# DeltaNet and a SiLU feed-forward layer in one kernel: chunk 0's norms, transposes, loads and scores rearranged

## The chip, the core and the metric

The kernel runs on one NeuronCore of a Trainium2 chip. The core has five engines that run their own instruction streams and meet at semaphores: TensorE (PE, matrix multiplication into PSUM; its weight loads appear as PEld), VectorE (DVE), ScalarE (ACT), GpSimd (POOL) and SyncE (SP), which here only issues DMA transfers. The metric is the time of one execution on the device in microseconds (us), as the median of several runs.

## What is computed

For each of 32 heads (batch 4, 8 heads, 768 tokens, head size 48), the keys are normalized and a 48x48 state is updated token by token:

```python
k_n = k / (norm(k) + 1e-6)
for t in range(S):
    y[t] = q[t] @ state
    state += beta[t] * outer(k_n[t], v[t] - k_n[t] @ state)
```

The result, seen as 3072 tokens of 384 numbers, goes through a feed-forward layer: `h = x @ w_in` (384 to 2048), `g = h * sigmoid(h)`, `out = g @ w_out` (2048 to 384). The two weight matrices arrive as 64-bit floats and are narrowed on the chip.

## The kernel before

**Chunks.** The 768 tokens are cut into six chunks of 128. In a chunk the token loop is replaced by matrices: the scores of keys against keys (`ap0`) and of keys against queries (`ap1`, masked to be causal), the inverse of a triangular matrix made of beta and the key scores, and products with the values. For the inverse each head's 128 tokens are split into four blocks of 32, so that DVE holds 128 blocks, one per partition, and inverts them all by rank-one updates. Chunk 0 has its own form, `invert_first` (L660): it inverts only the two 16x16 corners of each block, in 15 steps of two instructions (`rank`, L677, and the addition, L681), and then multiplies by beta over the squared norm, in the code `step` (L684).

**Joining the blocks.** DVE then turns the inverse twice: `low` (L691, 512 elements per partition) and `up` (L695, 1024). PE joins the corners to blocks of 64: `corner` (L718, which reads `low`), `turned` (L734, reads `up`), `straight` (L747, reads `up`), `merge_half` (L807). Between them ACT and DVE copy PSUM out (L545 is a copy by ACT and L548 one by DVE, whatever the tile); L725 on DVE adds the diagonal after `corner`. This runs as `joins(0)` for the first 64 tokens of the chunk and later, among other work, as `joins(1)` for the others.

**What comes ahead of it in chunk 0.** Keys are loaded by `load_k` (L142, six DMAs). POOL squares them (`square`, L385), DVE sums (`add_squares`, L389), and `norm_steps` finds the norm: a seed from the bits (L403), three Newton rounds (L409, L412, L413), the norm (L417, L418), its reciprocal (L419), times beta (L420), and four instructions for `spread` (L423), one per block of 32 rows. PE sums `spread` into place (`block_steps`, matmul `pg`, L446) and ACT copies it to `step` (L451). Meanwhile PE transposes the keys (`turn`, L501; evacuated by DVE in L513 or ACT in L515), forms the 32x32 blocks of scores (`first_blocks`, L1292), and DVE brings them to one block per partition with one transpose (`blocks_in`, L1299). The first product of the inverse is L669. beta is transposed by PE and copied by ACT (`beta_of`, L361 and L364).

**Orders written out by hand.** `pin` chains each compute instruction behind the one before on its engine, so every engine's order is the order of the Python text. `in_line` chains all DMAs of SP in the same way; within `deep`, each of them also waits for the end of the transfer two before it. An entry in the list `pace` makes the next DMA wait for one more instruction. `busy` issues a matmul `pw` (L348, 128x128 by 384) whose result nobody reads. In chunk 0, a list of words says what PE gets after which step of the inverse: `s2` is the key scores of batch 2, `u0` the transposes of the queries of batch 0, `w0` the query scores. After the joins, a long script of words orders everything until PE's feed-forward matmuls (`phid`, L1049) fill it; `narrow` (L232, L233 on ACT, L237, L241 on DVE, L245 on POOL) turns a piece of the weights to 32 bits.

**The SP queue before** holds, in this order: keys of chunk 0, queries of chunk 0 (tile `z`), pieces 0 and 1 of `w_in` (tile `raw`), keys of chunk 1, values of chunk 0 (`vf`), piece 2 of `w_in` (in the room of `w_out`), queries of chunk 1 (in the room of `sums_of_g`), pieces 4, 3, 6, 5 of `w_in`.

## Time and profile before

| | |
|---|---|
| median of 3 runs | 642.78 us (641.49 to 644.65) |
| the profiled execution's own time | 643.75 us |
| its span in the profile | 642.0 us |
| mean granted TensorE clock | 0.975 |
| instructions | 21886 |
| PE, DVE, ACT, POOL busy | 621.0, 402.2, 216.8, 94.5 us |
| read from and written to memory | 39.62 MB, 10.49 MB |

The profile is of one execution. A row of the timeline gives the start in us, the time from the first to the last instruction of a merged group, the engine, the line, what is written and read, the count, and in brackets how long the engine had been idle and which event ended that. "issue" there means that the profile shows nothing it waited for. PE's matmuls of 32-bit numbers appear twice each in the counts. A row of the windows gives the length of a stretch, the busy time of each engine in it with the number of instructions, the granted clock (1 is full speed), the share of DMA time and the GB/s.

### The profile page before, as it was taken

What the parts mean: (1) busy time and instruction counts of PE and PEld (TensorE: products, weight loads), DVE (VectorE), ACT (ScalarE), POOL (GpSimd) and SP (SyncE); (2) the same over time, 40 slices, a digit from 0 to 9 for tenths busy, and PEclk for the clock granted to TensorE, in tenths of its full rate; (3) what the DMA queues carried; (4) which work ended last, traced back from release to release, by engine and by line L of the source; (5) the groups of instructions that cost most, each with busy time, mean ns of one, the idle gap of its engine ahead of it and who ended that gap; (6) DMA issues with size and microseconds to landing.
All of it is one profiled execution on the core that took longest, in us unless ns stands there. A gap on an engine that the chain in (4) does not pass through costs nothing.

```text
span 642.0 us, 21886 instructions
## 1 busy us (share of the span) xinstructions
PE 621.0 (97%) x9642; PEld 547.7 (85%) x9642; DVE 402.2 (63%) x917; ACT 216.8 (34%) x512; POOL 94.5 (15%) x96
## 2 busy tenths in 40 slices
PE   6879999999999999999999999999999999999997
PEld 4767788666799978999989999989989989989997
DVE  5845888998774986564975563987563974212112
ACT  2655765251351122452122451122451122441120
POOL 5322730246010020010020010020002000000000
PEclk9758999999999999999999999999999999999999
DMA  9855454160369334269233269324173024100101
GB/s 171 184 120 186 146 123 106 50 149 3 84 127 158 59 76 49 59 135 160 39 92 43 48 137 147 60 75 61 29 148 80 1 74 61 38 16 1 26 0 26
DMA packets 141695, 53.69 MB, mean 84 GB/s; under 512 B 113296, under 2 KB 135056, under 8 KB 141600
## 3 DMA queue, kind: packets, MB, share of 16 engines
q1 hardware_dynamic: 141264, 52.14, 39.8%
q8 instruction: 76, 1.25, 0.8%
q10 hardware_dynamic: 336, 0.15, 0.1%
q14 instruction: 19, 0.16, 0.1%
HBM read 39.62 MB, written 10.49 MB: 78 GB/s over the span
## 4 chain that ended last, share of the span: by engine, by line
PE 71%; DVE 11%; DMA 7%; SPq 6%; issue 2%; ACT 2%; POOL 0%; DVEq 0%; POOLq 0%
PE phid L1049 27%; PE px L1156 13%; PE py L1156 10%; PE po L1084 7%; DVE rank L628 4%; DVE x L633 3%; PE pz L841 2%; PE pa L530 2%; PE ph L829 2%; SPq L142 2%; SPq L197 2%; PE pyc L922 2%; PE pyc L909 2%; DVE sums_of_g L1138 1%; PE pu L861 1%
## 5 line engine op out<-in xcount | busy, mean ns | idle before, releaser
L1049 PE MATMUL phid<-xT,w_in 128*128 128x256 f32 x1152 | 258.9, 383 | 0.1
L1049 PEld LDWEIGHTS phid<-xT,w_in 128*128 128x128 f32 x1152 | 217.0, 191 | 30.7 <-issue 1.3
L1059 ACT ACTIVATE gT<-phid 128x512 f32<-128x512 f32 x88 | 52.6, 598 | 143.1 <-PE phid L1049 136.5
L628 DVE SCALAR_TENSOR_TENSOR rank<-g,step,x 128x31 f32<-128x31 f32 (+15 forms) x124 | 49.8, 401 | 36.9 <-DMA g<-blocks 33.5
L1138 DVE TENSOR_TENSOR sums_of_g<-gT 128x384 f32<-128x384 f32 (+1 forms) x60 | 29.7, 514 | 56.7 <-ACT gT L1059 46.1
L1156 PE MATMUL py<-w_out,sums_of_g 128*128 128x192 f32 x320 | 56.8, 329 | 0.0
L1156 PE MATMUL px<-sums_of_w,sums_of_g 128*128 128x192 f32 x320 | 56.6, 329 | 0.0
L1156 PEld LDWEIGHTS px<-sums_of_w,sums_of_g 128*128 128x128 f32 x320 | 52.2, 190 | 0.5
L1156 PEld LDWEIGHTS py<-w_out,sums_of_g 128*128 128x128 f32 x320 | 52.2, 190 | 0.4
L633 DVE TENSOR_TENSOR x<-x,rank 128x31 f32<-128x31 f32 (+15 forms) x124 | 42.5, 343 | 4.3
L468 POOL TENSOR_TENSOR vf<-vf,n_slot 128x768 f32<-128x768 f32 x10 | 14.7, 1482 | 173.2 <-DMA vf<-in_v_dram 173.1
L868 DVE TENSOR_TENSOR state<-state,pu 48x384 f32<-48x384 f32 x44 | 24.3, 552 | 21.0 <-PE pu L861 20.0
L545 ACT COPY xT<-pyc 48x128 f32<-48x128 f32 (+2 forms) x126 | 32.7, 260 | 1.7
L489 DVE STREAM_TRANSPOSE kq<-stage 128x512 f32<-128x512 f32 x28 | 28.3, 1116 | 4.7 <-DMA stage<-in_q_dram 4.6
L1156 PE MATMUL px<-sums_of_w,gT 128*128 128x192 f32 x160 | 28.4, 329 | 0.0
L1156 PE MATMUL py<-w_out,gT 128*128 128x192 f32 x160 | 28.4, 329 | 0.0
L1156 PE MATMUL px<-w_out,gT 128*128 128x192 f32 x160 | 28.0, 327 | 0.0
L841 PEld LDWEIGHTS pz<-vf,xi 64*64 64x64 f32 x768 | 25.0, 142 | 3.2 <-issue 2.2
L551 POOL COPY g<-x 64x256 f32<-64x256 f32 x4 | 5.0, 1243 | 152.1 <-DVE x L636 152.1
L1156 PEld LDWEIGHTS px<-w_out,gT 128*128 128x128 f32 x160 | 26.4, 190 | 0.5
L841 PE MATMUL pz<-vf,xi 64*64 64x48 f32 x768 | 26.6, 226 | 0.0
L1156 PEld LDWEIGHTS py<-w_out,gT 128*128 128x128 f32 x160 | 26.1, 190 | 0.3
(197 smaller groups left out, 827.7 us busy)
## 6 DMA issues: line engine op xcount, KB each, us to landing
vf<-in_v_dram SPq DMA_DIRECT2D x48, 96.0 KB, 2.9
out_dram<-o SPq DMA_DIRECT2D x42, 96.0 KB, 2.2
w_out<-in_moe_w_in_dram SPq DMA_DIRECT2D x12, 256.0 KB, 3.5
sums_of_w<-in_moe_w_out_dram SPq DMA_DIRECT2D x8, 384.0 KB, 3.8
blocks<-ap SPq DMA_DIRECT2D x40, 64.0 KB, 1.9
g<-blocks SPq DMA_DIRECT2D x5, 512.0 KB, 3.8
kb<-in_k_dram SPq DMA_DIRECT2D x12, 192.0 KB, 4.6
kb<-in_k_dram SPq DMA_DIRECT2D x24, 96.0 KB, 4.5
```

The source lines that it names most:

```text
L468: pin(nc.gpsimd.tensor_tensor(out=vf, in0=vf, in1=of, op=ALU.mult))
L489: pin(nc.vector.transpose(out=kqs[c, b][:, :, j, :].rearrange("p a (i m) -> p a m i", i=T), in_=src.rearrange("p a (m d) -> p a m d", d=D) ...
L545: return pin(nc.scalar.copy(to, of))
L628: pin(nc.vector.scalar_tensor_tensor(out=tv, in0=g[:, 0:m, m : m + 1].to_broadcast([P, m, n]), scalar=step[:, m : m + 1], in1=x[:, m : m + ...
L633: yield pin(nc.vector.tensor_tensor(out=x[:, 0:m, m:T], in0=x[:, 0:m, m:T], in1=tv, op=ALU.add))
L841: yield pin(nc.tensor.matmul(pz[rows, n * D : (n + 1) * D], lhsT=xis[g][rows, u * H + 2 * p + e, :], rhs=vfs[c][rows, hf, g * HB + u, p, : ...
L868: pin(nc.vector.tensor_tensor(out=to, in0=to, in1=by_heads(pu[of]), op=ALU.add))
L1049: pin(nc.tensor.matmul(ph[:, j * GT : (j + 1) * GT], lhsT=w_in[:, a, (2 * f + j) * P : (2 * f + j + 1) * P], rhs=xTs[c, hf][:, a, :], star ...
L1059: pin(nc.scalar.activation(out=hidden_of(c, hf, f), in_=ph[:], func=ACTF.Silu, scale=-0.5 if in_blocks(c) else 0.5))
L1084: pin(nc.tensor.matmul(pos[i][:, 0:DM], lhsT=hidden_of(0, hf, f // 2)[:, at : at + C], rhs=w_outs[f // HFF][:, f % HFF, :], start=(f == 0) ...
L1138: pin(nc.vector.tensor_tensor(out=sums_of_g[:, k, fs], in0=of[0], in1=of[1], op=op))
L1156: pin(nc.tensor.matmul(to, lhsT=at, rhs=quarter(f, *b) if isinstance(b, tuple) else sums_of_w[b][:, f], start=start and f == 0, stop=f == ...
```

## The change

All of it is in chunk 0, except that the norm's formula is shared by all chunks.

- `norm_steps`: another seed constant, one Newton round with other constants and one cubic round, of which the norm itself comes out. Chunk 0 then squares the norm, takes the reciprocal, and multiplies `spread` by it in one instruction of 128x128; ACT has put minus beta into `spread` ahead of that in four copies (`beta_of`). The other chunks keep their reciprocal and their five instructions behind it.
- The square of the last batch's keys goes from POOL to ACT.
- The two clearings of `xi` on POOL go ahead of the squares.
- The two transposes write `low` and `up` in order; `corner`, `turned` and `straight` read them with a stride of 32 numbers.
- Queries of chunk 0 are issued later in the text, and their first DMA waits for the sums of the third batch (`pace`). Values of chunk 0 go between pieces 0 and 1 of `w_in`, ahead of the keys of chunk 1.
- The key scores of batch 0 go ahead of the norms' `pg` on PE, those of batch 1 behind `blocks_in`; the word list of the inverse is another one; the narrowing of piece 0 begins at its eleventh step.
- Four more `pw` matmuls in all: eight instead of four. One is ahead of the last batch's `first_blocks`, one ahead of `pg` behind the scores of batch 0, one ahead of the scores of batch 1, and two are among the inverse's steps; the one behind the scores of batch 1 is gone.

The core of the diff:

```diff
-    load_q(0)
...
-        pin(nc.scalar.activation(
-            out=beta_tok[:, c, :].rearrange("p (n e) -> p e n", e=2),
-            in_=pb[:, 0:BH].rearrange("p (e n) -> p e n", e=2), func=ACTF.Copy,
-        ))
+        for j in range(NB if c == 0 else 1):
+            rows = slice(T * j, T * (j + 1)) if c == 0 else ALL_ROWS
+            to = spread[rows, j, :] if c == 0 else beta_tok[:, c, :]
+            pin(nc.scalar.mul(
+                to.rearrange("p (n e) -> p e n", e=2), pb[rows, 0:BH].rearrange("p (e n) -> p e n", e=2),
+                -1.0 if c == 0 else 1.0,
+            ))
...
+        if (c, b) == (0, 3):
+            pin(nc.scalar.activation(out=squared[c, b], in_=kb, func=ACTF.Square))
+        else:
+            pin(nc.gpsimd.tensor_tensor(out=squared[c, b], in0=kb, in1=kb, op=ALU.mult))
...
-        for _ in range(3):
-            yield pin(nc.vector.scalar_tensor_tensor(
-                out=t, in0=ss, scalar=-0.5, in1=root, op0=ALU.mult, op1=ALU.mult
+        yield pin(nc.vector.scalar_tensor_tensor(out=t, in0=ss, scalar=-k, in1=root, op0=ALU.mult, op1=ALU.mult))
+        yield pin(nc.vector.tensor_tensor(out=t, in0=t, in1=root, op=ALU.mult))
+        yield pin(nc.vector.scalar_tensor_tensor(
+            out=r, in0=t, scalar=k * 2.38924456, in1=root, op0=ALU.add, op1=ALU.mult
+        ))
+        yield pin(nc.vector.scalar_tensor_tensor(out=t, in0=ss, scalar=0.5, in1=r, op0=ALU.mult, op1=ALU.mult))
+        yield pin(nc.vector.tensor_tensor(out=root, in0=t, in1=r, op=ALU.mult))
+        yield pin(nc.vector.scalar_tensor_tensor(
+            out=r, in0=root, scalar=-5.0 / 3.0, in1=root, op0=ALU.add, op1=ALU.mult
+        ))
+        yield pin(nc.vector.scalar_tensor_tensor(out=t, in0=r, scalar=1.25, in1=t, op0=ALU.add, op1=ALU.mult))
+        yield pin(nc.vector.tensor_scalar(
+            out=n[:], in0=t, scalar1=3.0, scalar2=1e-6, op0=ALU.mult, op1=ALU.add
+        ))
+        if c == 0:
+            yield pin(nc.vector.tensor_tensor(out=t, in0=n[:], in1=n[:], op=ALU.mult))
+            yield pin(nc.vector.reciprocal(out=r, in_=t))
+            yield pin(nc.vector.tensor_tensor(
+                out=spread[:], in0=spread[:], in1=r.unsqueeze(1).to_broadcast([P, NB, BH]), op=ALU.mult
             ))
...
-        low = sum_room[:, AT_LOW : AT_LOW + BH * Q].rearrange("p (n s) -> p n s", s=Q)
+        low = sum_room[:, AT_LOW : AT_LOW + BH * Q].rearrange("p (s n) -> p s n", s=Q)
-        pin(nc.vector.transpose(out=low.rearrange("p n s -> p s n"), in_=x[:, 0:Q, :]))
+        pin(nc.vector.transpose(out=low, in_=x[:, 0:Q, :]))
...
-                        rhs=low[rows[j], n, :], start=True, stop=True,
+                        rhs=low[rows[j], :, n], start=True, stop=True,
...
-    for b in range(B):
+    for t in xis:
+        pin(nc.gpsimd.memset(t, 0.0))
+    for b in range(3):
         square(0, b)
     block_room(0)
     for b in range(2):
         turn(0, b, 0, (A, CC)[b % 2], b % 2 == 0)
-    for b in range(B):
+    square(0, 3)
+    for b in range(2):
         add_squares(0, b)
-    for b in range(2):
         first_blocks(b)
     for b in range(2, B):
         turn(0, b, 0, (A, CC)[b % 2], False)
+        add_squares(0, b)
+        if b == 2:
+            pace.append(pins[seen_on])
     first_blocks(2)
     beta_of(0)
+    busy(1)
     first_blocks(3)
-    busy(0)
-    for t in xis:
-        pin(nc.gpsimd.memset(t, 0.0))
+    load_q(0)
+    first_score(0)
+    busy(1)
     first_sizes = norm_steps(0)
-    go(first_sizes, 18)
+    go(first_sizes, 12)
     step = block_steps(0)
     go(first_sizes, 99)
     blocks_in()
...
     fetch_w_in(0)
+    load_v(0)
     fetch_w_in(1)
     load_k(1)
-    load_v(0)
+    busy(1)
+    first_score(1)
     for c in range(1, NCH):
         beta_of(c)
-    for b in range(2):
-        first_score(b)
-    busy(1)
     fetch_w_in(2)
     deep(load_q, 1)
...
-    begin(("in", 0))
...
-        for word in ["s2 u0 u1", "", "w0", "s3", "w1", "u2", "", "u3 w2", "", "", "", "", "w3", "", "", "", "", "", "", "", "", ""][n].split():
+        for word in [
+            "s2", "n s3", "u0", "u1 w0", "w1", "u2", "u3", "w2", "w3", "n", "N", "", "", "", "", "", "",
+        ][n].split():
```

Here `n` is one `busy`, and `N` begins the narrowing of piece 0.

## The prediction

> **What bounds the kernel now.** I read the page first, then the windows by stage, then the timeline of the first 60 us.
>
> ```profile
> span 642.0 us, 21886 instructions
> PE 621.0 (97%) x9642; PEld 547.7 (85%) x9642; DVE 402.2 (63%) x917; ACT 216.8 (34%) x512; POOL 94.5 (15%) x96
> PEclk9758999999999999999999999999999999999999
> PE 71%; DVE 11%; DMA 7%; SPq 6%; issue 2%; ACT 2%; POOL 0%; DVEq 0%; POOLq 0%
> ```
>
> PE is busy for 97% of the span, and its clock is granted in full except in the first slices of 16 us. The windows (columns: length, PE, PEld, DVE, ACT, POOL busy, clock, DMA share, GB/s) say where the rest is.
>
> ```profile
> 17.60:26.20 8.60, 8.36 (x210) 6.70 (x209) 7.58 (x30) 6.47 (x18) 0.19 (x1) 0.67 0.92 157
> 30.10:47.00 16.90, 12.12 (x429) 11.49 (x431) 8.24 (x18) 7.68 (x16) 6.62 (x5) 0.50 0.53 138
> 47.00:60.00 13.00, 11.98 (x291) 10.26 (x285) 7.20 (x11) 7.68 (x14) 3.69 (x2) 0.89 0.54 164
> 120.00:642.00 522.00, 516.15 (x7158) 461.04 (x7156) 313.06 (x709) 152.36 (x374) 51.73 (x46) 1.00 0.37 71
> ```
>
> From about 47 us on PE is full, and the change leaves its work there as it is. So the change is worth as many us as PE enters that stage earlier. Ahead of it the order is keys, norms, inverse, joins, and up to the joins DVE carries it:
>
> ```profile
> 9.71 0.55 DVE L389 TENSOR_REDUCE ss<-sq 128x8 f32<-128x384 f32 x1 [0.89 <-POOL sq L385]
> 10.49 0.55 DVE L389 TENSOR_REDUCE ss<-sq 128x8 f32<-128x384 f32 x1 [0.23 <-POOL sq L385]
> 11.08 0.30 DVE L403 TENSOR_SCALAR seed<-ss 128x32 uint32<-128x32 uint32 x1
> 11.42 0.19 DVE L409 SCALAR_TENSOR_TENSOR nt<-ss,seed 128x32 f32<-128x32 f32 x1
> ...
> 13.46 0.19 DVE L417 TENSOR_TENSOR nt<-nr,ss 128x32 f32<-128x32 f32 x1
> ...
> 13.90 0.35 DVE L419 RECIPROCAL nr<-n 128x32 f32<-128x32 f32 x1
> 14.36 0.19 DVE L420 TENSOR_TENSOR nt<-nr,beta_tok 128x32 f32<-128x32 f32 x1
> 14.59 0.77 DVE L423 SCALAR_TENSOR_TENSOR spread<-nr,nt 32x32 f32<-32x32 f32 x4
> 15.39 1.25 DVE L1299 STREAM_TRANSPOSE sums_of_w<-blocks 128x1024 f32<-128x1024 f32 x1
> 16.75 0.69 DVE L669 TENSOR_TENSOR sums_of_w<-sums_of_w,step 128x512 f32<-128x512 f32 x1
> ...
> 21.89 0.29 DVE L681 TENSOR_TENSOR sums_of_w<-sums_of_w,rank 128x128 f32<-128x128 f32 x1
> ```
>
> No row of DVE from the seed to L669 has an idle time in brackets: one instruction behind the other sets the start of the inverse.
>
> **The change, part by part.** *The last square on ACT.* DVE's fourth sum came 0.23 us late behind POOL; with ACT squaring beside POOL it follows the third at once. Gain 0.23 us. The square is 384 elements per partition and goes where ACT was idle (first row below); if that cover is gone, L515 moves by about 0.45 us, half the 0.91 us that ACT needs for 768 elements (ACT, L232, further down).
>
> *Norms.* Now 18 instructions from 11.08 to 15.36 us (14.59 + 0.77), 4.28 us. After: 12. The seed takes 0.34 us to the next start; the nine starts from 11.42 to 13.46 give 0.227 us each, and nine of the other instructions are of that kind (2.04 us); the reciprocal takes 0.46 us (13.90 to 14.36); the product of 128x128 is bounded below by an instruction of 32 elements, 0.19 us, and above by two of L681, 0.6 us; I take L681 itself, the same size, 0.29 us and 0.03 to start. Sum 3.16 us, gain 1.12 us. Together DVE is ready 1.35 us earlier, at 14.0 us, and L669 could start at 15.4.
>
> *What stands in its way.* L669 also needs `step`, which PE and ACT make, and the change puts more ahead of that on PE.
>
> ```profile
> 9.87 1.07 ACT L515 COPY kq<-pt 128x512 f32<-128x512 f32 x2 [1.64 <-PE pt L501]
> 11.47 1.85 POOL L1328 MEMSET xi<- 128x1024 f32 x2
> 13.39 0.84 PE L1292 MATMUL blocks<-kq 48*32 48x32 f32 x58 [1.76 <-issue]
> 15.51 0.61 PE L446 MATMUL pg<-pick,spread 128*128 128x32 f32 x2 [1.28 <-DVE spread L423]
> 16.15 0.19 ACT L451 COPY step<-pg 128x32 f32<-128x32 f32 x1 [4.47 <-PE pg L446]
> 17.65 1.99 PE L530 MATMUL pa<-kq 48*64 48x64 f32 x64
> 19.56 1.65 PE L348 MATMUL pw<-state,ident 128*128 128x384 f32 x2
> 20.21 0.91 ACT L232 ACTIVATE w_in<-raw 128x768 f32<-128x768 f32 x1
> 34.05 0.69 PE L734 MATMUL pl<-sums_of_w 32*32 32x32 f32 x19 [2.01 <-issue]
> ```
>
> Behind the third batch's blocks (11.4 us) PE will issue `pw`, the last 64 block matmuls, the scores of batch 0, `pw`, `pg`. At the durations above, most of them under a halved clock, that is 1.65 + 0.93 (0.84 x 64/58) + 1.0 (half of L530) + 1.65 + 0.61 = 5.84 us, `step` at 17.5 us and L669 0.75 us later than now. If the stall of 1.76 us at 13.39 stays as well, it is 2.5 us later. At the full clock the 5.84 halve to 2.9, and DVE decides, 1.35 us earlier. I take the full clock for the first three (half of 3.58 us), as the window around them was granted it, the half clock for the rest, and no stall, because the queries no longer load at that time: 11.4 + 1.79 + 2.26 = 15.5, `step` at 15.8, L669 at about 15.95. **Gain 0.8 us**; ends +1.35 and -2.5.
>
> *Four copies of beta by ACT* take the place of one. They come after L515 and end by about 12.5 us, ahead of the product at 13.7: no cost, and up to 0.3 us if they don't. *The clearings of `xi`*, 1.85 us, go into POOL's wait for the keys; POOL also loses a square, so nothing waits for them.
>
> *The two transposes in order.*
>
> ```profile
> 27.23 1.06 DVE L691 STREAM_TRANSPOSE sums_of_w<-sums_of_w 128x512 f32<-128x512 f32 x1
> 28.15 1.91 DVE L695 STREAM_TRANSPOSE sums_of_w<-sums_of_w 128x1024 f32<-128x1024 f32 x1
> 29.94 1.45 DVE L725 SCALAR_TENSOR_TENSOR sums_of_w<-pl,second,pick 64x128 f32<-64x128 f32 x4
> 30.41 1.63 PE L734 MATMUL pl<-sums_of_w 32*32 32x32 f32 x40 [0.43 <-DVE sums_of_w L725]
> ```
>
> Written with a stride they take 2.1 and 1.9 ns per element. L1299, which writes in order and reads with a stride, takes 1.25 us for 1024, 1.2 ns each. So `low` goes to 0.62 us and `up` to 1.25: 1.10 us less, and L725 and the joins start that much sooner. If only the reading mattered, `up` would stay at 1.91 and the gain be 0.44; that is the case in which the change doesn't do what it says. **I take 1.1 us.** L725 can't start before `corner` is through, but that begins earlier too.
>
> *Strided reading on PE.* 640 of the matmul records (L718, L734, L747 in both joins) now read `low` or `up` with a stride of 32 numbers. No row shows PE reading SBUF with a stride; bounds are nothing, or less, and a doubling. I take nothing: these matmuls move 16 or 32 columns.
>
> *Loads.* The queries waited for nothing (5.98 us below); now they wait for the third sum, which ends at 10.26. All of SP's queue behind them slides by 4.3 us.
>
> ```profile
> 5.98 4.01 SPq L142 DMA_DIRECT2D z<-in_q_dram  x6
> ...
> 31.33 8.29 SPq L142 DMA_DIRECT2D sums_of_g<-in_q_dram  x6
> 39.67 8.06 SPq L292 DMA_DIRECT2D w_out<-in_moe_w_in_dram  x6
> w_out<-in_moe_w_in_dram SPq DMA_DIRECT2D x12, 256.0 KB, 3.5
> 47.65 0.47 PEld L501 LDWEIGHTS pt<-ident,sums_of_g 128*128 128x128 f32 x4
> 56.04 0.89 ACT L232 ACTIVATE w_in<-w_out 128x768 f32<-128x768 f32 x1
> ```
>
> Against 4.3 us of delay and 1.9 us of earlier use, 6.2 in all: the queries of chunk 1 are through in half at about 35 + 3 us and used at 47.65, 9 us of slack. Piece 3 of the weights, issued by 47.7 and landing 3.5 us later, is used at 56.04: 4.8 us, so ACT would wait 1.4 us for it. What is queued behind it on ACT is the rest of the narrowing and the activations of `phid`, which wait for PE anyway. I price it at nothing; 1.4 us if that cover is gone.
>
> *`pw`.* Two of the four added ones stand ahead of `pg` and are in the sum; the others lie under the inverse, where DVE is ahead of PE.
>
> **Sum:** 0.8 + 1.1 = 1.9 us from the profiled execution, whose span of 642.0 and the 1.73 us around it make 643.75; it becomes 641.85. That execution is 0.97 us above the median, so the forecast is 642.78 - 1.9 = **640.9 us**.
>
> **Rivals.** *Warm clock.* The joins ran at a clock of 0.50 (30.10 to 47.00). The same 320 instructions at the two clocks (same columns, DVE and ACT behind PE):
>
> ```profile
> 28.00:43.00 15.00, 6.03 (x320) 5.33 (x320) 3.92 (x10) 2.17 (x6) 0.57 0.58 141
> 50.00:70.00 20.00, 4.83 (x320) 4.06 (x320) 3.95 (x10) 2.17 (x6) 0.91 0.52 162
> ```
>
> They cost 1.2 us more in the first, and the other matmuls up to 47 us (some 6 us of busy time) could gain as much again. If the added `pw` hold the clock, 1 to 4 us come on top: 637 to 640 us, middle 638.4. Against it: the last `pw` stands at the tenth step, about 21 us, some five us ahead of the joins. The Trainium skill (TensorE: Matmul & The Clock Gate, Part 1) says that the clock is given after a busy window of about 3.4 us and taken after an idle one; by it the gap before the joins would cost the clock again, and the phase differs between runs. The trace agrees that the clock comes in stages, 0.67, 0.50, 0.89 in the windows.
>
> *PE ahead of `pg`.* The stall or the half clock holds `step`, and the norms' gain turns to a loss of up to 2.5 us: with the transposes 642 to 644.2 us. For it: both lie in the rows; against it: the queries are out of the way.
>
> *Strided reads, the slower side.* The records of one `joins` have 6.03 and 4.83 us, 10.9 in all. If strided reads lengthen them by more than a sixth (1.9 of 10.9), the gain is gone; by 47%, the kernel is 0.5% slower; doubled, it is 640.9 + 10.9 = 651.8. The Trainium skill (SBUF — State Buffer, Door 1: The DMA port swizzle, the note on cachelines) speaks against the change here: an access that leaves a 16-byte line for another pays a penalty, so that 32-bit numbers a stride of 32 apart would all pay. DVE's two transposes agree with it (1.06 us for 512), L1299's strided read does not, though it reads PSUM; for PE no run here shows it yet.
>
> *Late loads.* The 4.3 us reach ACT or the joins where I saw slack: 642 to 645.
>
> **How the numbers follow.** Forecast 0.47 (639.6 to 642), warm clock 0.22, PE ahead of `pg` 0.13, strided reads 0.10, late loads 0.08. About 0.5%, 3.2 us, is what a measurement of this kernel can tell from no change. Faster by more: most of the warm clock and the forecast's best end (+1.35, +1.1 and the 2.01 us stall gone), 0.32. Slower by more (over 646): most of the strided reads and the tail of the two others, 0.14. The rest, 0.54, is no difference. The range of 637.3 to 645.5 leaves out the warmest clock and the strided reads that cost.
>
> **What would show it.** Right: DVE's seed before 11 us and 12 instructions to about 14; L669 near 16; the transposes at 0.6 and 1.25 us; `phid` starting about 2 us earlier. Wrong: `pg` waiting behind PE's own work with DVE idle before L669; records of L718, L734, L747 over 6 us in the first joins at the same clock; ACT waiting for a DMA at L232; a granted clock of 1 between 30 and 45 us.

## The result and the profile after

The changed kernel takes 648.72 us (median of 22 runs, 644.1 to 652.15) where the kernel before, run beside it, takes 644.41 (22 runs, 641.49 to 649.62). The ratio is **1.0052, with a 95% interval of 1.0034 to 1.0071**: slower by about 3.4 us, where 1.9 us less had been forecast. It is the ratio of the means, 648.28 and 644.91 us; the medians lie further apart. The profiled execution of the changed kernel is one of 650.37 us, 1.65 above its median.

The page of the changed kernel:

```profile
span 648.6 us, 21880 instructions
PE 624.8 (96%) x9650; PEld 549.8 (85%) x9650; DVE 398.9 (61%) x896; ACT 217.5 (34%) x516; POOL 93.6 (14%) x95
PEclk9958999999999998999999999999999999999999
...
q8 instruction: 76, 1.25, 0.8%
```

DVE has 3.3 us less to do, PE 3.8 us more; q8, of which more below, is by its count of packets the queue that brings PE's instructions. The timelines of DVE and of PE show that the head of chunk 0 does what was wanted of it up to `low`:

```profile
10.06 0.18 DVE L411 TENSOR_SCALAR seed<-ss 128x32 uint32<-128x32 uint32 x1
...
12.76 0.29 DVE L433 TENSOR_TENSOR spread<-spread,nr 128x128 f32<-128x128 f32 x1
12.99 1.25 DVE L1317 STREAM_TRANSPOSE sums_of_w<-blocks 128x1024 f32<-128x1024 f32 x1
14.81 0.69 DVE L689 TENSOR_TENSOR sums_of_w<-sums_of_w,step 128x512 f32<-128x512 f32 x1 [0.57 <-ACT step L471]
...
25.30 0.71 DVE L711 STREAM_TRANSPOSE sums_of_w<-sums_of_w 128x512 f32<-128x512 f32 x1
25.93 1.97 DVE L715 STREAM_TRANSPOSE sums_of_w<-sums_of_w 128x1024 f32<-128x1024 f32 x1
```

```profile
14.26 0.30 PE L466 MATMUL pg<-pick,spread 128*128 128x32 f32 x2
...
32.30 0.95 PE L752 MATMUL pl<-sums_of_w 32*32 32x32 f32 x26 [2.58 <-issue]
37.95 1.00 PE L765 MATMUL pl<-sums_of_w 32*32 32x32 f32 x57 [2.95 <-issue]
```

The clock, too, is granted in full up to the joins (windows of the changed kernel, then of the kernel before, where it is 0.77):

```profile
6.70:30.60 23.90, 19.94 (x723) 15.26 (x722) 19.99 (x57) 13.47 (x43) 9.55 (x11) 1.00 0.81 165
30.60:47.70 17.10, 11.10 (x386) 10.50 (x389) 6.60 (x13) 7.38 (x15) 4.19 (x3) 0.50 0.43 97
```

```profile
6.70:30.60 23.90, 18.37 (x684) 15.06 (x683) 20.31 (x60) 12.05 (x38) 10.49 (x12) 0.77 0.95 194
```

The first product of the inverse (L689, formerly L669) starts at 14.81 us instead of 16.75, `low` at 25.30 instead of 27.23. `low` takes 0.71 us instead of 1.06, but `up`, written in order, 1.97 instead of 1.91. Then the lead of 1.93 us goes. In the joins PE twice stands idle with nothing to wait for that the profile names, 2.58 and 2.95 us; before it was 2.01 (quoted in the prediction) and, in the waits of PE from 24 to 47 us of the kernel before,

```profile
PE pl L747 <- issue: 1.0, 1, 1.0
```

The joins' own records (windows of tile `pl`, first and second joins; before: 6.03 and 4.83 us) are longer as well:

```profile
26.00:43.00 17.00, 6.21 (x320) 5.60 (x320) 3.90 (x10) 2.17 (x6) 0.64 0.63 128
50.00:73.00 23.00, 6.09 (x320) 5.21 (x320) 3.94 (x10) 2.17 (x6) 0.93 0.56 180
```

SP issues the queries 3.6 us later than before (9.59 against 5.98) and piece 3 of the weights 8.6 us later (48.28 against 39.67), and ACT waits for the weights (timelines of SP and ACT, then ACT's waits from 50 to 75 us):

```profile
9.59 3.84 SPq L142 DMA_DIRECT2D z<-in_q_dram  x6
...
31.45 1.58 SPq L291 DMA_DIRECT2D w_out<-in_moe_w_in_dram  x3
37.75 10.49 SPq L142 DMA_DIRECT2D sums_of_g<-in_q_dram  x6
48.28 8.70 SPq L291 DMA_DIRECT2D w_out<-in_moe_w_in_dram  x6
...
60.06 0.92 ACT L231 ACTIVATE w_in<-w_out 128x768 f32<-128x768 f32 x1 [2.30 <-DMA w_out<-in_moe_w_in_dram]
```

```profile
ACT w_in L231 <- DMA w_out<-in_moe_w_in_dram: 3.9, 2, 2.3
```

The first copy `xi<-px` of the joins starts at 40.51 us (before 39.95): a lead of 1.93 us at `low` has become a lag of 0.56, and those 2.5 us are what the two stalls grew by (3.0 to 5.5). The first `kq<-phid` starts at 104.92 (before 100.76). In the 3.6 us lost between the two copies the profile shows the second joins with 1.3 us more of records and ACT's waits for the weights, of which the kernel before has none. So of the 6.6 us between the two profiled executions 4.2 lie ahead of 105 us, and 2.5 in the long stage behind it.

Where those 2.5 us go can be read as well. PE does not set the pace of that stage alone: near 241 us, in both kernels, it waits for the DMA `xe<-low`, which ends a chain of moves, transfers and DVE's inverse of a later chunk (timeline of PE of the kernel before, then of the changed one):

```profile
241.93 1.25 PE L783 MATMUL py<-xe,ap 32*32 32x32 f32 x124 [0.79 <-DMA xe<-low]
243.11 2.87 PE L1156 MATMUL px<-w_out,gT 128*128 128x192 f32 x16
```

```profile
247.12 1.25 PE L801 MATMUL py<-xe,ap 32*32 32x32 f32 x124 [0.24 <-DMA xe<-low]
248.30 4.55 PE L1174 MATMUL px<-w_out,gT 128*128 128x192 f32 x16
```

From the first `kq<-phid` to the first of these rows it is 141.17 us before and 142.20 now, 1.0 more. The 16 matmuls behind it then take 4.55 us instead of 2.87, and the granted clock from 240 to 280 us is 0.96 instead of 1.00. Together that is 2.7 us. In 11 of the 20 profiles of this document these 16 matmuls take 4.5 us or more; in the other 9, both profiles of the kernel before among them, they take 2.87. Whether the change makes the slower case more frequent can't be told from one profile of each kernel.

### The profile page after: what moved, and what is told of

Read it like the earlier page. It is cut to its first block, busy times and chain, and to the rows that moved or that the text cites. A ratio compares the mean times of both kernels' runs of the same rounds, so it can differ in the third digit from the quotient of the medians.

```text
span 648.6 us, 21880 instructions
## 1 busy us (share of the span) xinstructions
PE 624.8 (96%) x9650; PEld 549.8 (85%) x9650; DVE 398.9 (61%) x896; ACT 217.5 (34%) x516; POOL 93.6 (14%) x95
## 3 DMA queue, kind: packets, MB, share of 16 engines
q8 instruction: 76, 1.25, 0.8%
## 4 chain that ended last, share of the span: by engine, by line
PE 77%; DMA 10%; DVE 6%; SPq 5%; issue 1%; ACT 1%; POOL 0%; DVEq 0%; POOLq 0%; ACTq 0%
PE phid L1067 32%; PE px L1174 15%; PE py L1174 11%; PE po L1102 7%; DMA w_out<-in_moe_w_in_dram 4%; PE pa L550 3%; PE pz L859 2%; DVE rank L648 2%; SPq L142 2%; DVE x L653 2%; PE ph L847 2%; PE pyc L927 1%; PE pyc L940 1%; DMA sums_of_g<-in_q_dram 1%; PE pu L879 1%; DMA kb<-in_k_dram 1%
## 5 line engine op out<-in xcount | busy, mean ns | idle before, releaser
L648 DVE SCALAR_TENSOR_TENSOR rank<-g,step,x 128x31 f32<-128x31 f32 (+15 forms) x124 | 49.7, 401 | 35.1 <-DMA g<-blocks 31.7
L1174 PE MATMUL px<-w_out,gT 128*128 128x192 f32 x160 | 29.7, 341 | 0.0
L1174 PEld LDWEIGHTS px<-w_out,gT 128*128 128x128 f32 x160 | 28.1, 200 | 0.5
```

The source lines that it names most:

```text
L648: pin(nc.vector.scalar_tensor_tensor(out=tv, in0=g[:, 0:m, m : m + 1].to_broadcast([P, m, n]), scalar=step[:, m : m + 1], in1=x[:, m : m + ...
L1174: pin(nc.tensor.matmul(to, lhsT=at, rhs=quarter(f, *b) if isinstance(b, tuple) else sums_of_w[b][:, f], start=start and f == 0, stop=f == ...
```

## The experiments

All are compared with the kernel before on the same chip, in five rounds each. "pw" is the idle matmul of `busy`. The table gives the ratio and, of the one profiled execution, its own time and the starts of two copies by ACT, the first `xi<-px` (the joins done) and the first `kq<-phid`.

| run | what differs | ratio (95%) | own time | `xi` | `kq` |
|---|---|---|---|---|---|
| before | | 1 | 643.75 | 39.95 | 100.76 |
| after | the whole change | 1.0052 (1.0034 to 1.0071) | 650.37 | 40.51 | 104.92 |
| e1_loads_as_before | after, loads of before | 1.0044 (1.0022 to 1.0065) | 645.15 | 38.20 | 101.16 |
| e2_only_loads | before, loads of after | 1.0015 (0.9995 to 1.0035) | 647.39 | 39.78 | 101.56 |
| e3_no_wait | after, queries don't wait | 1.0075 (1.0048 to 1.0101) | 648.34 | 41.52 | 104.99 |
| e4_old_transposes | after, transposes of before | 1.0028 (1.0006 to 1.0049) | 648.09 | 40.11 | 101.90 |
| e5_norms_and_order | after, loads and transposes of before | 1.0050 (1.0026 to 1.0075) | 648.72 | 41.44 | 102.62 |
| e6_only_norms | before, norms of after | 1.0022 (0.9991 to 1.0053) | 650.58 | 40.71 | 100.20 |
| e7_moves_first | e5, moves ahead of `g<-blocks` | 1.0065 (1.0041 to 1.0089) | 649.80 | 42.41 | 100.97 |
| e8_only_transposes | before, transposes (one of a later chunk by mistake) | 1.0025 (1.0001 to 1.0049) | 650.25 | 40.37 | 102.72 |
| e9_weights_first | after, pieces 0 to 2 first | 1.0053 (1.0029 to 1.0077) | 645.60 | 38.61 | 100.08 |
| e10_before_weights_first | before, piece 2 early | 0.9994 (0.9971 to 1.0017) | 643.03 | 39.34 | 99.63 |
| e11_four_pw_less | after, four pw less | 1.0039 (1.0016 to 1.0062) | 644.83 | 39.44 | 99.56 |
| e12_all_but_strides | e7 and pieces first | 1.0036 (1.0010 to 1.0062) | 649.59 | 41.91 | 101.72 |
| e13_before_4_tiny | before, 16 PE instructions more | 1.0023 (1.0004 to 1.0043) | 644.61 | 40.21 | 100.82 |
| e14_no_strides_no_pw | e4 and e11 together | 1.0024 (1.0003 to 1.0044) | 646.24 | 38.41 | 100.83 |
| e15_transposes_alone | before, the two transposes | 1.0039 (1.0013 to 1.0064) | 646.42 | 39.49 | 100.17 |
| e16_before_again | nothing | 1.0007 (0.9991 to 1.0022) | 640.97 | 39.79 | 97.23 |
| e17_before_dve_late | before, DVE 4.7 us late | 1.0047 (1.0027 to 1.0067) | 644.98 | 42.98 | 102.24 |
| e18_after_dve_late | after, DVE 4.4 us late | 1.0062 (1.0029 to 1.0094) | 646.95 | 41.77 | 102.74 |

Two things bound what can be read from it. A ratio is good to between 0.15 and 0.33%, 1 to 2 us. And e16, the same kernel as before, has a profiled execution 2.8 us shorter, so that a microsecond or two in a single profile is no verdict on a kernel.

### The loads: e1, e2, e3

The first theory was that the late loads, which the forecast had priced at nothing, were most of the loss.

```diff
 # e1 (after, without the wait and in the old order); e2 is the reverse, on the kernel before
+    load_q(0)                      # ahead of w_in
...
-        if b == 2:
-            pace.append(pins[seen_on])
...
-    load_v(0)
     fetch_w_in(1)
     load_k(1)
+    load_v(0)
 # e3: only the two lines of pace go
```

> The changed kernel with the loads of before: queries of chunk 0 straight behind the keys without a wait, values of chunk 0 behind the keys of chunk 1. All else as changed. Theory (late loads: the wait on the third sum pushes SP's whole queue back, and the joins and the narrowing of the weights meet it): the loss goes and the earlier start of the joins stays, ratio to before 0.995 to 0.999 (640 to 643 us), no wait of ACT for a DMA at the narrowing of piece 3. Rival A (PE's instruction stalls come from the added matmuls and their place): ratio stays at 1.003 or more. Rival B (PE reads low and up with a stride): ratio stays at 1.002 or more.

> The kernel before with the new order of loads alone (queries of chunk 0 behind the third sum, values of chunk 0 between pieces 0 and 1). Theory (late loads): slower by 4 to 7 us, ratio 1.006 to 1.011, with ACT waiting about 2 us for a DMA at the narrowing of piece 3. Rivals A and B: within 1.5 us of before, ratio below 1.003.

> The changed kernel with the queries of chunk 0 at once behind the keys (the wait on the third sum taken away), values still ahead of piece 1. Theory (late loads, by the wait): SP's queue is 4 us earlier again and most of the loss goes, ratio 0.996 to 1.000. If the place of the values counts as well, 1.002 to 1.004. Rivals A and B: 1.004 to 1.006, as the changed kernel.

The theory fell as the main cause. The loads alone cost the kernel before 0.15%, and giving them back to the changed kernel takes off 0.08% (e1); neither can be told from nothing. The wait by itself may even help: without it the ratio is 1.0075, though its interval overlaps that of the changed kernel. In its profile PE stalls ahead of the last blocks and the product starts at 16.50 us instead of 14.81, as the forecast's rival had it (timeline of PE, then of DVE, e3):

```profile
13.62 0.72 PE L1310 MATMUL blocks<-kq 48*32 48x32 f32 x60 [1.37 <-issue]
```

```profile
16.50 0.69 DVE L689 TENSOR_TENSOR sums_of_w<-sums_of_w,step 128x512 f32<-128x512 f32 x1 [0.73 <-ACT step L471]
```

e1 shows a second place where a lead can end. It comes to the joins' end 1.75 us ahead of before (38.20) and still has it at 97 us; there PE waits for chunk 0's moves, which stand in SP's queue behind `g<-blocks` (timeline of PE; the windows from 97 to 119 us of e1, and of the kernel before):

```profile
98.05 6.24 PE L1068 MATMUL phid<-xT,w_in 128*128 128x256 f32 x20 [1.82 <-DMA xT<-part]
```

```profile
97.00:119.00 22.00, 20.95 (x89) 18.20 (x90) 20.78 (x45) 7.60 (x11) 3.21 (x2) 0.92 0.30 72
```

```profile
97.00:119.00 22.00, 21.90 (x140) 18.91 (x130) 20.46 (x49) 10.09 (x17) 1.96 (x1) 1.00 0.34 76
```

Before, PE is full here, 21.90 of 22.00 us, at a clock of 1.00. Where PE comes earlier it waits, and the clock falls: 0.92 over 22 us is 3.5 us at half speed, which costs as much again as the wait. The Trainium skill (TensorE: Matmul & The Clock Gate, Part 1) has the clock decided in windows of about 3.4 us, and the trace agrees with that length, though the wait ahead of it, 1.82 us, was shorter.

### The transposes: e4, e8, e15

```diff
 # e4 undoes this in the changed kernel; e15 does it alone in the kernel before
-        low = sum_room[...].rearrange("p (n s) -> p n s", s=Q)
+        low = sum_room[...].rearrange("p (s n) -> p s n", s=Q)
-        pin(nc.vector.transpose(out=low.rearrange("p n s -> p s n"), in_=x[:, 0:Q, :]))
+        pin(nc.vector.transpose(out=low, in_=x[:, 0:Q, :]))
-                        rhs=low[rows[j], n, :], start=True, stop=True,
+                        rhs=low[rows[j], :, n], start=True, stop=True,
...                                 # up in the same way
```

> The changed kernel with low and up laid out as before, so that DVE writes with a stride and PE reads in order. Rival B (strided reading on PE costs about 1.3 us in each of the two joins): 2 to 2.5 us less than the changed kernel, ratio to before 1.001 to 1.002, and weight loads of the turned step back from 145 to about 114 ns. Late loads and rival A: no better than the changed kernel, 1.004 to 1.007.

> The kernel before with the two transposes written in order and low and up read with a stride, nothing else. If strided reads cost PE: low 0.71 us instead of 1.06, up 1.9 to 2.0 as before, each of the two joins 0.4 to 1.3 us longer on PE at the same clock, ratio 1.0025 (1.001 to 1.004). Rival, the forecast's term: 0.4 to 1.1 us gained, ratio 0.998 to 0.9995.

> The kernel before with chunk 0's two transposes in order and the strided reading, nothing else (the run e8_only_transposes had changed a transpose of the later chunks by mistake). If strided reads cost 1.5 us: ratio 1.0025 (1.001 to 1.004), low 0.71 us, up 1.9 to 2.0, the second joins some 6.1 us of PE records instead of 4.83. Rival, the forecast's term: ratio 0.998 to 0.9995.

e8's edit of `up` met the transpose of the later chunks instead of chunk 0's, so it computes other values; chunk 0's `low` and the strides of all of PE's reads are as meant. e15 is the clean one. They point the same way: +0.39% alone (e15, whose interval leaves out 1) and +0.25% (e8, barely so), and 0.24% less when undone (e4), which by itself is within the error of the two ratios. Windows of tile `pl` of e15 (the kernel before: 6.03 and 4.83), then a row of the tile's groups in e15 and the same in the kernel before (duration ns min/median/max):

```profile
26.00:43.00 17.00, 6.12 (x320) 5.50 (x320) 3.95 (x10) 2.17 (x6) 0.70 0.61 150
50.00:73.00 23.00, 5.83 (x320) 5.04 (x320) 3.95 (x10) 2.17 (x6) 0.93 0.49 157
```

```profile
L732 PEld LDWEIGHTS pl<-sums_of_w x128: 126/145/149, 30.7 to 61.0; 32*32 32x32 f32 x128
```

```profile
L734 PEld LDWEIGHTS pl<-sums_of_w x128: 101/114/153, 30.4 to 61.8; 32*32 32x32 f32 x128
```

A weight load of 32x32 numbers with a stride of 32 takes 145 ns instead of 114, and the second joins 5.83 us of records instead of 4.83 at the same clock of 0.93. In exchange DVE wins 0.35 us on `low` and nothing on `up`, whose transpose reads with a stride in both kernels.

### Norms and order: e5, e6, and the moves: e7, e12

```diff
 # e5: after with e1's loads and e4's transposes
 # e6: before + norm_steps, beta_of, the square on ACT, xi cleared early; words, pw and PE's order of before
 # e7: e5, and in the script of words and in block_in:
-        "... l2 p f s2 l2 f l4 f r2 f p2 v ..."
+        "... l2 f s2 p l2 f l4 f r2 f p2 v ..."
-        in_line(nc.sync.dma_start(out=g, in_=there[:]))
+        issue(g, there[:], c == 1)     # by ACT's queue for chunk 1
 # e12: e7, and
     fetch_w_in(1)
+    fetch_w_in(2)
     load_k(1)
     load_v(0)
```

> The changed kernel with the loads and the two transposes of before: shorter norms, the square on ACT, the new order and the added pw on PE remain. If the strided reads and the late loads cost what their two undoings gave (0.24% and 0.08% of the time), the ratio is 1.002 (1.000 to 1.004): the lead of 2 to 3 us is there from 30 to 97 us and is lost behind 97 us, where phid waits about 2 us for its moves (xT<-part), and the clock falls for some 3.4 us. Rival, that the loss lies in the strided reads and the loads alone: the lead is kept and the ratio is 0.996 (2 to 3 us less).

> The kernel before with the shorter norms alone (formula, spread by ACT, the last square on ACT, xi cleared early); PE's order, pw, loads and transposes as before. If what the norms gain is lost at the moves at 97 us, the ratio is 1.000 to 1.002 with the lead of about 1 us gone by 102 us. Rival, that the new order and the added pw make the loss: the lead of 1 to 1.3 us is kept to the end, ratio 0.998. Third, that step is held by PE as the forecast feared: L669 no earlier than before and ratio 1.000.

> The kernel of the run e5_norms_and_order, with the moves xT<-part of chunk 0's second half ahead of g<-blocks in SP's queue, and that g<-blocks issued by ACT's queue. If PE's gap at 96 to 98 us and the clock behind it are what eats the lead: no gap there, phid from 96 us on at full clock, kq at 101 us still 2 us earlier than before, and the ratio 0.3 to 0.5% below that of e5_norms_and_order, 0.998 or less. Rival, that the lead is lost for another reason (PE full behind it anyway, g late): the gap closes and the ratio stays within 0.1% of e5_norms_and_order, or another wait takes its place.

> The changed kernel's norms and PE order, with the transposes and the early queries of before, pieces 0 to 2 of w_in ahead of the keys of chunk 1, and chunk 0's moves ahead of g<-blocks (the run e7_moves_first with the weights first). By the theory that the lead is lost to the supply in the joins, to the moves and to the strided reads: lead of 2 to 3 us from 47 us to 120 us, ratio 0.996 to 1.000. Rival, that the wait xe<-low at 240 us and stalls at other places take the lead back whatever happens ahead of them: ratio 1.001 to 1.006 like its siblings.

e5 is as slow as the whole change, and its interval leaves out 1, so norms and order together do not gain with the loads and transposes of before either, but lose. The timelines of DVE show what became of the lead at the head in these two executions. In e6 (first fence) the norms end at 13.41 us, 1.95 earlier, but DVE then waits 1.31 us for PE's block matmuls, and the product starts at 16.08, 0.67 earlier than before. In e5 (second) `pg` stands behind the scores under a halved clock, and the product starts at 17.80, a microsecond later than before:

```profile
13.12 0.29 DVE L434 TENSOR_TENSOR spread<-spread,nr 128x128 f32<-128x128 f32 x1
14.72 1.25 DVE L1318 STREAM_TRANSPOSE sums_of_w<-blocks 128x1024 f32<-128x1024 f32 x1 [1.31 <-PE blocks L1311]
...
16.08 0.69 DVE L690 TENSOR_TENSOR sums_of_w<-sums_of_w,step 128x512 f32<-128x512 f32 x1
```

```profile
17.80 0.69 DVE L690 TENSOR_TENSOR sums_of_w<-sums_of_w,step 128x512 f32<-128x512 f32 x1 [1.87 <-ACT step L472]
```

e7 and e12, with the same order and early queries, start it at 17.26 and 17.62; but e1, which is the same up to there, ran at the full clock and started it at 15.64, ahead of before. One profile does not tell how often this order starts late.

e7 closes the wait at 97 us, as expected: none of PE's waits from 90 to 110 us names `xT<-part` any more. The time does not follow (1.0065, against 1.0050, with overlapping intervals). So the wait at the moves is real, but closing it gains nothing that can be seen; in the profile of e7 PE waits longer near 241 us instead (3.0 us for `xe<-low` in all, 1.1 in e5). e12 ends within the rival's range too.

### The supply of instructions: e9, e10, e11, e13

What "issue" is in the joins can be read from the DMA queues. Counted in the traces, PE's longer idle times called issue begin behind its record 448, 704, 1216, 1472, 1728, 3264 or 7104, in whichever run (the prediction's stall of 1.76 us at 13.39 is the one at 448): all of these are a multiple of 256 plus 192. Queue q8 moved 76 packets of 16 KB in all (1.25 MB), and PE has some 19,440 records, counting matmuls, weight loads and semaphore instructions: a packet for 256. In the changed kernel PE goes on with a new 256 at 32.30 us; the packet for the next one does not come between 32.30 and 35.50 us, when weights fill the queues, but in the 0.2 us behind that, and PE goes on at 37.95. DMA queues of the changed kernel from 35.50 to 35.70 us, and of the kernel before from 35.1 to 35.3 (there PE resumes at 34.05, and the packet comes 1.1 us later):

```profile
q8 instruction: 1, 0.02, 33.0%
```

```profile
q8 instruction: 1, 0.02, 29.6%
```

In the first 50 us of the 20 profiles this packet starts 0.4 to 3.4 us after PE has begun the 256 ahead of it; in the joins it is 1.1 us in many of them and 3.3 in the changed kernel, and where PE stood waiting it went on some 2.4 us after the packet's start. In the first 75 us of the 20 profiles no 256 took less than 3.1 us. That is no limit of PE everywhere: near 444 us, behind matmuls of 192 columns, 256 pass in 1.8 us in the kernel before. The Trainium skill (Runtime: NRT & Kernel Launch, Instruction fetch mechanics) says the same of the blocks, 16 KiB for 256 instructions, and calls the cost of a boundary mostly hidden. The traces agree on the size; that the cost is hidden holds among the long `phid` matmuls and not in the joins.

```diff
 # e9 (after); e10 puts the same line into the kernel before; in both the later fetch_w_in(2) goes
     fetch_w_in(0)
-    load_v(0)
     fetch_w_in(1)
+    fetch_w_in(2)
     load_k(1)
+    load_v(0)
 # e11: four of the eight pw go (two busy(1), two words n); e13: behind busy(3), in the kernel before
+    for _ in range(4):
+        pin(nc.tensor.matmul(pw[:, 0:32], lhsT=ident[:], rhs=..., start=True, stop=True))
```

> The changed kernel with another order of loads alone: pieces 0, 1 and 2 of w_in, then the keys of chunk 1, then the values, so that piece 2 has landed when the joins begin. Theory of the supply: PE's idle time called issue in the joins is the wait for its own instructions, whose transfers (queue q8) stand behind the loads' packets. Then the two stalls of 2.58 and 2.95 us at L752 and L765 go to 0.5 to 1.5 us each, the first copy of xi<-px comes 2 to 4 us earlier than in the changed kernel, and the ratio is 1.000 to 1.003 instead of 1.005. Rival, that PE is held there by its own matmuls (the strided reads, the half clock): the stalls stay within 0.5 us and the ratio within 0.1% of 1.005.

> The kernel before with piece 2 of w_in ahead of the keys of chunk 1 in SP's queue, nothing else. By the theory of the supply the stalls of 2.01 and 1.03 us in the joins lose 1 to 2 us together and the ratio is 0.997 to 0.999, less what the waits at 97 and 240 us take back (then 1.000). Rival, that the loads don't matter there: stalls as before, ratio 1.000 with the values and keys of chunk 1 late by some 2 us for nothing.

> The changed kernel without four of its eight pw (the one behind the scores of batch 0, the one ahead of the scores of batch 1 and the two among the inverse's steps). If pw cost nothing, as forecast: ratio within 0.1% of that of the changed kernel. If they move PE's instruction stream so that it runs dry at about 180 us (1.66 us idle there in the changed kernel, nothing in the kernel before): that idle time falls below 0.8 us, ratio 1.002 to 1.004. Rival, that they hold the clock ahead of the joins: half the clock from 20 us instead of 30.6, corner 1 us later, ratio 1.006 to 1.008.

> The kernel before with four matmuls more, 128x128 by 32 and read by nobody, behind the first three pw at 3 to 6 us, where PE waits for the keys: 16 instructions more on PE, no work of any size. Theory of the supply: PE's stream is cut into pieces of 256 instructions, and the 16 move the cut near 178 us into the burst of small matmuls (pyc); there PE gets an idle time called issue of 0.8 to 1.8 us that the kernel before has not, and the ratio is 1.001 to 1.003. Rival, that small extra work at the start is nothing: no such idle time, ratio 1.000.

With the new order of the loads the stalls are shorter, as the theory has it. Waits of PE from 24 to 47 us in e9 (2.6 and 2.9 in the changed kernel) and in e10 (2.0 and 1.0 before):

```profile
PE pl L752 <- issue: 1.7, 1, 1.7
PE pl L765 <- issue: 1.3, 1, 1.3
```

```profile
PE pl L734 <- issue: 1.4, 1, 1.4
PE pl L747 <- issue: 1.0, 1, 1.0
```

e10's 1.4 says little: with the old order that stall is 2.2 us in e16 and 1.1 in e15. e9's joins end 1.9 us earlier than those of the changed kernel. And the time stays: 1.0053. That is the part of the expectation that failed. e10 is 0.06% under before, which is no difference.

Behind the joins the theory did worse. The changed kernel runs dry near 182 us, which the first profile of the kernel before does not (waits of PE from 110 to 642 us, then a line of the same view of e16):

```profile
PE pyc L940 <- issue: 1.4, 1, 1.4
```

```profile
PE phid L1049 <- issue: 0.7, 1, 0.7
```

So in e16 the kernel before runs dry at the same count of records too, for half as long. With four pw less (e11) PE waits 0.51 us there and the ratio is 1.0039, in the range expected, but no further from 1.0052 than the error. e13, which was to bring that stall into the kernel before by 16 instructions, is 0.23% slower and **has no such stall**: its waits from 110 us on are

```profile
PE py L783 <- DMA xe<-low: 1.2, 2, 0.8
PE ph L829 <- issue: 0.3, 1, 0.3
```

So the time expected came without the mechanism, which is luck: that a shift of the stream by 16 puts the cut into a bad place is not shown, and why e13 is slower is open. Its lower bound, 1.0004, is barely above no change.

### Both suspects, the kernel again, and a known delay: e14, e16, e17, e18

```diff
 # e17 (before) and e18 (after), between the norms and the inverse's first transpose
     go(first_sizes, 99)
+    for _ in range(4):
+        pin(nc.vector.memset(sum_room[:, AT_UP : AT_UP + BH * T], 0.0))
     blocks_in()
```

> The changed kernel with the transposes of before and four pw less, both suspects undone at once; norms, PE order and late loads stay. If the two are most of the loss and add up (0.24% and 0.13%): ratio 1.0015 (1.000 to 1.003). Rival, that the loss has other grounds (norms and order against the supply and the moves): ratio 1.003 to 1.005 as in the changed kernel.

> The kernel before once more, unchanged, as a measure of what two profiles and two sets of runs of one kernel differ by. All theories: ratio 1.000 within 0.2%. The profile says how far the stalls in the joins, the wait at 240 us and the clock stages move by themselves: the theory that single profiles differ by 1 to 3 us between 240 and 280 us without a cause in the kernel expects up to that; if it repeats the first profile within 0.5 us at every milestone, differences of 1 us in the other profiles are theirs.

> The kernel before with four clearings of 128x1024 on DVE (about 1 us each, of a room that is written later anyway) between the norms and the first transpose of the inverse: L669 starts some 4 us later and nothing else changes. By the prediction's premise, every us at the head is a us at the end: ratio 1.006 (1.005 to 1.008). If the head is held by PE's instructions in the joins, by the moves at 97 us and by the clock, part of the 4 us vanishes: ratio 1.000 to 1.003.

> The changed kernel with the same four clearings at the same place. By the premise the same 4 us: ratio 1.011 to 1.012. If the lead of the changed kernel at the head is worth nothing, the first 2 us of delay cost nothing here: ratio 1.005 to 1.009, and less added than in e17_before_dve_late.

e14 takes half of the loss away, at 1.0024; since e4 alone had 1.0028, the four pw add nothing that can be told. The delays bear on the main question, what a start at the head is worth at the end. Timeline of DVE and the largest of PE's waits from 20 to 50 us, in e17:

```profile
15.77 0.91 DVE L1334 MEMSET sums_of_w<- 128x1024 f32 x1 [0.28 <-issue]
...
21.47 0.69 DVE L669 TENSOR_TENSOR sums_of_w<-sums_of_w,step 128x512 f32<-128x512 f32 x1
```

```profile
PE pl L718 <- DVE sums_of_w L691: 4.5, 1, 4.5
```

The same two views of e18:

```profile
19.18 0.69 DVE L689 TENSOR_TENSOR sums_of_w<-sums_of_w,step 128x512 f32<-128x512 f32 x1
```

```profile
PE pl L736 <- DVE sums_of_w L711: 4.5, 1, 4.5
PE pl L752 <- issue: 1.4, 1, 1.4
PE pl L765 <- issue: 1.0, 1, 1.0
```

In the kernel before, a start of the inverse 4.72 us later (21.47 instead of 16.75) costs 0.47% of 643.53 us, 3.0 us (1.7 to 4.3). In the changed kernel 4.37 us (19.18 instead of 14.81) add 0.10%, 0.6 us; with both intervals that is -1.8 to 3.1, so not all of it. The joins' stalls are 2.4 us there instead of 5.5, perhaps because later joins meet fewer of the loads. **The changed kernel, whose inverse starts at 14.81 us, and e17, where it starts at 21.47, take the same time** within what is measured (1.0052 and 1.0047).

## Why the prediction was wrong, step by step

- **The step that failed is the premise**: "the change is worth as many us as PE enters that stage earlier". It was read from PE being full behind 47 us in the kernel before. That holds for PE as it came, not for a PE that comes earlier, and near 241 us not even for PE as it came: there the kernel before waits 2.2 us for `xe<-low`. In the changed kernel the lead of 1.93 us does not live to that stage: the waits for instructions in the joins, 5.5 us instead of 3.0, take all of it and more. In its variants a lead that outlives the joins meets the moves at 97 us (1.82 us in e1, and the clock behind it). The delays put a price on the head: 4.4 us for 0.6 at the end in the changed kernel (e18, -1.8 to 3.1), 4.7 for 3.0 in the kernel before (e17). At these prices the 1.9 us of the sum would be worth 0.3 or 1.2 us; that is an estimate from the two ratios, and no run shows that an advance counts as a delay does.
- *Last square and norms*: more came of it on the spot than its best end. L689 starts 1.94 us earlier; 0.8 was taken, with ends of +1.35 and -2.5. The seed alone starts 1.02 us earlier (10.06 instead of 11.08), where 0.23 was counted. PE's stall of 1.76 us ahead of `pg` is gone, and the clock from 6.7 to 30.6 us is 1.00, so `step` was hardly late (0.57 us).
- *Transposes*: "I take 1.1 us" was wrong; it is 0.29 (2.97 to 2.68 us). `low` had 0.71 for the 0.62 foreseen, `up` 1.97 for 1.25. L1299, the row that 1.25 was taken from, reads PSUM. `up` reads SBUF with a stride in both kernels, and to take the stride out of the write alone gained nothing. It is the named case in which the change doesn't do what it says.
- *Strided reading on PE*, "I take nothing": this is the term mis-sized. It and norms with order (e5, 0.50%, with the four pw) are the two parts that a run shows to lose by themselves. PE's records in both joins went from 10.86 to 12.30 us, +13%, and the time by 0.24 or 0.39%, 1.5 or 2.5 us (e4, e15). The rival had the mechanism and the sixth from which it eats the gain; with the gain gone, less is enough. The Trainium skill's note on cachelines (SBUF — State Buffer, Door 1: The DMA port swizzle), cited there, speaks of a penalty for such an access, and the 145 ns against 114 agree with it; the argument from 16 or 32 columns did not hold.
- *Loads*: ACT was said to wait 1.4 us for piece 3 and waited 2.30, 3.9 in all. Cost in time: 0.15% (-0.05 to 0.35), not told from nothing (e2).
- *The stall of 2.01 us* that was counted into the best end didn't go. It begins at a count of 256 instructions like the others, and it grew to 2.58.
- *`pw`* priced at nothing: 0.13% less without four (e11), 0.04% beside the transposes (e14 against e4); neither is resolved.
- *Rivals.* Warm clock: full up to 30.6 us, then 0.50 up to 47.7 us as before; it fell where it mattered. Over the whole run the changed kernel has the higher clock, 0.982 as the mean of its 22 executions against 0.978 in the 35 of the kernel before beside e9 to e12, so the clock as a whole is not its loss; among executions of one kernel 0.001 less goes with some 0.4 to 0.6 us more. PE ahead of `pg`: not in the changed kernel, but in the profiles of e3, e5, e7 and e12, where the wait of the queries is missing; not in that of e1, where it is missing too. Strided reads: a part of the loss. Late loads: waits of ACT, and nothing that can be told in the time.

What adds up: of 0.52%, the transposes are 0.24 or 0.39, and that the strided reads in the joins lengthen them is measured. The parts don't sum: taken one by one onto the kernel before, transposes, loads and norms with order and pw make 0.39, 0.15 and 0.50. Open is why norms, order and late loads still cost 0.24% with the transposes undone and four pw gone (e14, 1.0003 to 1.0044) when they should at worst be worth nothing. In the profiles the time from the first `kq<-phid` to the end is 543.0 us in the kernel before (543.7 in e16), 545.5 in the changed one and 545.4 in e14; the half clock behind the wait near 241 us is most of that in the changed kernel, and e14 has it as well (4.55 us for the 16 matmuls). But e11 has 545.3 us without it, so it is not the whole account, and whether the change or the moment of an execution brings it on, no run here decides. No version here beats the kernel before; e10 equals it.

## What to carry to other kernels

An engine that is busy for 99% of a stage is full for the time at which it now arrives; before counting a gain ahead of it as a gain at the end, look for the places in it where it waits all the same, and delay the head by a known amount to see what comes out. A layout that turns one engine's strided access into another's should be priced on both sides from rows with the same memory and stride, and where there is none, measured alone. In streams of very small matmuls, look for idle time without a releaser at equal counts of instructions, and for the transfers that run then; to move them shortened the stalls here (e9), though not the kernel's time.

## What the runs showed of the hardware

- PE's instructions come in packets of 256. With full queues a packet started up to 3.3 us after PE had begun the 256 ahead of it, and PE stood idle for up to 2.95 us (changed kernel, in the joins). In the first 75 us of the 20 profiles no 256 took less than 3.1 us.
- A 32x32 weight load from SBUF with a stride of 32 numbers takes 145 ns, in order 114 (medians of e15 and of the kernel before); the 32x16 matmuls of `corner` that read so 183 instead of 178.
- DVE's transpose of 1024 numbers per partition within SBUF takes 2.03 us with a strided write (L606 before), 1.97 with a strided read (L715 after) and 1.91 with both (L695 before); with the strided read from PSUM it takes 1.25 (L1299).
- A wait of PE of 1.82 us was followed by some 3.5 us at half the clock (e1, 97 to 119 us).
